# Gated linear attention and an MLP on one core: inputs turned by VectorE, four array tiles for the states, the MLP by 256 tokens and in quarter blocks at the start

## The chip, the cores and the metric

The kernel runs on one core of a Trainium2 chip. Its engines are TensorE (PE, matrix products), VectorE (DVE), ScalarE (ACT), GpSimd (POOL) and SyncE (SP), which here only issues DMAs. The metric is the device time of one execution in microseconds, as the median of several runs.

## The reference

The inputs are q, k, v and f_logit, each of 4 batches, 8 heads, 768 tokens and 48 values a head, and the MLP's weights w_in (384 x 2048) and w_out (2048 x 384), in 64-bit floats. The attention keeps a state per head, and the MLP takes the eight heads' outputs of a token side by side as its 384 inputs:

```
f = 1.0 / (1.0 + np.exp(-f_logit))
state = np.zeros((B, H, D, D), dtype=np.float32)
for t in range(S):
    state = f[:, :, t, :, None] * state + np.einsum('bhd,bhe->bhde', k[:, :, t], v[:, :, t])
    y[:, :, t] = np.einsum('bhd,bhde->bhe', q[:, :, t], state)
...
h = x @ w_in
g = h * (1.0 / (1.0 + np.exp(-1.702 * h)))
return (g @ w_out).astype(np.float32)
```

## The kernel before

**Units.** The 3072 tokens are cut into twelve units of 256 tokens, three to a batch. For each unit `attention` (L177) makes a list of parts, each a piece of the program with a kind, T or W. The MLP works on two units at a time (TM = 512 tokens, L399).

**Parts of a unit.** Six T parts turn f, q and k (`turn`, L187): `load_raw` (L143) brings them with tokens on partitions, in runs of 48 floats padded to 64. TensorE transposes 128x128 blocks with an identity (L195), four to a part, and ScalarE brings the result from PSUM, with a sigmoid for f (L201) and as a copy for q and k (L203), so that channels lie on partitions: two heads on 128 partitions, four such pairs side by side, 1024 columns in all. GpSimd multiplies f over pairs, fours and so on up to 64 tokens (L210). VectorE makes q times f (L214). Then come a first and a second W part and four W parts by `level` (L310). Each makes scores on TensorE (`score`, L220, matmul at L224); VectorE scales q and k up one level (`promote`, L251, at L260) and masks the scores while it takes them from PSUM (`evacuate`, L239, at L244); ScalarE copies keys (L264); TensorE adds the products with v (`add`, L269, at L273) into the PSUM tile py. Two T parts turn k back (`turn_k`, L324). A W part makes the sums of k and v for four chunks of 64 tokens (L347), and VectorE forms the states from them (L360 to L365). The last W part adds the states' share to py (L378): head h of a pair reads partitions of h and writes columns of h, so it is on two tiles of the array, while scores and adds use all four. ScalarE copies py to yT (L384), and ten DMAs put yT into xT (L390) with the MLP's inputs in their order on partitions.

**v.** `load_v` (L152) copies v to a buffer in DRAM with all heads of a token side by side, and then loads it seven times in the orders that the levels need (vl), and once in plain order (vn). There is one vl.

**MLP.** `mlp_h` (L401): for each of 16 blocks of 128 hidden values three matmuls (L412), a sigmoid on ScalarE (L418) and a product on VectorE (L419) into g. `mlp_o` (L422): for each 128 tokens sixteen matmuls (L429), a copy by ScalarE (L435) and a DMA out (L437). The hidden tiles, ph and po, share three PSUM banks.

**Weights.** They come as 64-bit floats in 24 pieces of w_in (256 columns) and 16 of w_out (384 columns). `load_weights` (L111) issues the DMA, of which three pieces can be in flight, and turns the bits into 32-bit floats with one ScalarE instruction (L130) and six on VectorE (L131 to L137).

**Order.** TensorE's instructions run in the order in which the program writes them (L81). The order on the other engines and on SP is made at compile time by a planner, which issues what is ready by its own costs, first the one that the program writes first. `merge` (L441) writes TensorE's order: after each part it takes a share of the fill, a list of MLP matmuls or of weight pieces. Units 0 and 1 take weight pieces as fill (L506, L508). The second half of unit 1 and unit 2 have the h matmuls of the first 512 tokens, in two halves of 256 (L509 to L514). From unit 3 on each unit takes one unit's worth of MLP, which lies a LAG behind (L515 to L520).

Of the kernel before, what the change touches and what calls it, by code (L numbers as in the profile page):

```python
# [24 lines left out]
def kernel(  # L25
# [44 lines left out]
    FG = 4  # L70
    NA = NP * U
# [16 lines left out]
    at = [wp.tile([P, 64], I32, tag="bits", name=f"at{j}", bufs=3) for j in range(2)]  # L88
# [8 lines left out]
    raw = const.tile([P, 3, NG, H, HS], F32, name="raw")  # L97
    for j in range(3):
        nc.vector.memset(raw[:, j, :, :, D:], 0.0)
# [3 lines left out]
    v_toks = [tc.dram_tile([U, DM], F32, name=f"v_tok{j}") for j in range(2)]  # L103

    WI, WO = 256, 384
    pieces_in = [(w_in[:, c, f:f + WI], moe_w_in[c * P:(c + 1) * P, f:f + WI])
                 for f in range(0, DFF, WI) for c in range(NK)]
    pieces_out = [(w_out[:, c, e:e + WO], moe_w_out[c * P:(c + 1) * P, e:e + WO])
                  for c in range(NFF) for e in range(0, DM, WO)]

    def load_weights(n, dst, src):  # L111

        w = dst.shape[1]
        if moe_w_in.dtype == F32:
            nc.sync.dma_start(out=dst, in_=src)
            return
        bits = wp.tile([P, w, 2], I32, tag="bits", name=f"bits_{n}", bufs=3)
        nc.sync.dma_start(out=bits.rearrange("p c two -> p (c two)"), in_=src.bitcast(I32))
# [24 lines left out]
    def load_raw(n):  # L143
        b, s0 = n // NU, n % NU * U
        for j, src in enumerate((f_logit, q, k)):
            for g in range(NG):
                nc.sync.dma_start(
                    out=raw[:, j, g, :, :D],
                    in_=src[b, :, s0 + g * G:s0 + (g + 1) * G, :].rearrange("h p d -> p h d"),
                )  # L150

    def load_v(n):  # L152
# [9 lines left out]
        for u, (m, half) in enumerate(V_HALF):  # L162
            nc.sync.dma_start(
                out=vl[:, u], in_=v_tok.rearrange("(n two m) e -> two n m e", two=2, m=m)[half]
            )
# [11 lines left out]
    def attention(n, loaded, xT, x0):  # L177
# [7 lines left out]


        def turn(j, a0):  # L187
            if not t:
                t["F"] = att.tile([P, NA], F32, tag="F", name=f"F_{n}")
                t["X"] = att.tile([P, 3, NA], F32, tag="X", name=f"X_{n}")  # L190
                t["tot"] = att.tile([P, NA], F32, tag="tot", name=f"tot_{n}")
            pt = ps.tile([P, 2, NG, P], F32, tag="tr", name=f"t{'fqk'[j]}_{n}_{a0}")
            for a in range(2):
                for g in range(NG):
                    nc.tensor.transpose(  # L195
                        pt[:, a, g, :], raw[:, j, g, 2 * (a0 + a):2 * (a0 + a + 1), :].rearrange("p h d -> p (h d)"), ident
                    )
            cols = slice(a0 * U, (a0 + 2) * U)
            src = pt.rearrange("p a g t -> p (a g t)")
            if j == 0:  # L200
                nc.scalar.activation(t["F"][:, cols], src, AF.Sigmoid)  # L201
            else:
                nc.scalar.copy(t["X"][:, 2 * (j - 1), cols], src)  # L203
            if j == 0 and a0:
                t["tms"], off = [t["F"]], 0
                for m in LEV:
                    nb = NA // (2 * m)
                    t2 = t["tms"][-1].rearrange("p (n two) -> p n two", two=2)
                    tn = t["tot"][:, off:off + nb]
                    nc.gpsimd.tensor_tensor(tn, t2[:, :, 0], t2[:, :, 1], ALU.mult)  # L210
                    t["tms"].append(tn)
                    off += nb
            if j == 1:
                nc.vector.tensor_tensor(t["X"][:, 1, cols], t["X"][:, 0, cols], t["F"][:, cols], ALU.mult)  # L214

        for j in range(3):
            for a0 in (0, 2):
                part("T")(lambda j=j, a0=a0: turn(j, a0))

# [9 lines left out]
        def tokens(j, m, half):  # L229
            return lambda h, x: t["X"][rows(h), j, x:x + G].rearrange("p (n two m) -> p n two m", two=2, m=m)[:, :, half, :]  # L230

        def keys(l):
            return lambda h, x: t["Kc"][rows(h), x // 2:x // 2 + 64]

# [16 lines left out]
        def promote(l):  # L251
# [5 lines left out]
            X = t["X"]  # L257
# [11 lines left out]
        def add(u, A, dst, start=False):  # L269

            for a in range(NP):
                for h, g in TILES:
                    nc.tensor.matmul(  # L273
                        dst(h, g, a), lhsT=t["vl"][g * 64:(g + 1) * 64, u, (2 * a + h) * D:(2 * a + h + 1) * D],
                        rhs=A(h, g, a), start=(start and a == 0), stop=False, skip_group_check=True,
                    )

        def half(m, hf):
            return lambda h, g, a: t["py"][rows(h), g, a, :].rearrange("p (n two m) -> p n two m", two=2, m=m)[:, :, hf, :]
# [5 lines left out]
        def _():  # L285
            t["vl"], t["vn"] = loaded()
            sc = scores()
            score(
                sc.rearrange("p h (a t) -> p h a t", a=NP), lambda h, x: t["X"][rows(h), 2, x:x + G:2],
                lambda h, x: view(t["X"], x, [[NA + 1, 2], [2, 64]])[rows(h)],  # L290
# [5 lines left out]
        def _():  # L296
            sc = scores()
            s4 = sc.rearrange("p h (s a t) -> p s h a t", s=2, a=NP)
            score(s4[:, 0], lambda h, x: t["X"][rows(h), 2, x + 1:x + G:2], lambda h, x: t["X"][rows(h), 0, x + 1:x + G:2])
# [5 lines left out]
                lambda h, g, a: t["py"][rows(h), g, a, :], start=True,  # L305
# [18 lines left out]
        def turn_k(a0):  # L324
            if a0 == 0:
                t["kn"] = att.tile([P, NP, NG, P], F32, tag="kn", name=f"kn_{n}")
            pt = ps.tile([P, 2, NG, P], F32, tag="tr", name=f"tkn_{n}_{a0}")
            for a in range(2):
                for g in range(NG):
                    x = (a0 + a) * U + g * G  # L330
                    nc.tensor.transpose(pt[:, a, g, :], t["X"][:, 2, x:x + G], ident)  # L331
# [37 lines left out]
        def _():  # L369
# [4 lines left out]
            for c in [1, 2, 3, 0][:NC - first]:  # L374
                for a in range(NP):
                    for h in range(2):
                        x = a * U + c * C
                        nc.tensor.matmul(  # L378
                            py[rows(h), c // 2, a, c % 2 * C:(c % 2 + 1) * C], lhsT=t["before"][c][rows(h), a],
                            rhs=t["X"][rows(h), 1, x:x + C], start=False, stop=True, skip_group_check=True,  # L380
                        )
            yT = att.tile([P, NP, NG, G], F32, tag="yT", name=f"yT_{n}", bufs=2)
            for h in range(2):
                nc.scalar.copy(yT[rows(h)].rearrange("p a g t -> p g a t"), py[rows(h)])  # L384
                for a in range(NP):
                    f0, f1 = (2 * a + h) * D, (2 * a + h + 1) * D
                    while f0 < f1:
                        end = min(f1, (f0 // P + 1) * P)
                        r0 = h * HS + f0 - (2 * a + h) * D
                        nc.sync.dma_start(  # L390
                            out=xT[f0 % P:f0 % P + end - f0, f0 // P, x0:x0 + U],
                            in_=yT[r0:r0 + end - f0, a].rearrange("p g t -> p (g t)"),
                        )
# [156 lines left out]
```

## Time and profile before

| | us |
|---|---|
| median of 3 runs | 797.74 |
| lowest, highest | 796.32, 798.1 |
| the profiled execution | 798.2 |
| its span, first to last instruction | 796.3 |
| TensorE busy | 722.1 |
| VectorE busy | 339.0 |
| ScalarE busy | 204.4 |
| GpSimd busy | 39.5 |

The profile is of one execution. Times within it are counted from the span's start. A line such as L429 is a line of the kernel; an arrow shows which tile an instruction writes and reads; a number after x is how many there are. Each fp32 matmul of the program shows as two instructions. Ends of matmuls are modelled, so their pace is read from the start of one to the start of the next.

### The profile page before, as it was taken

How to read it: one execution, taken by the hardware profiler on the slowest of the kernel's cores; microseconds unless marked ns; L12 is line 12 of the kernel's file. 1: busy time of each engine (PE TensorE's matmuls, PEld its weight loads, DVE VectorE, ACT ScalarE, POOL GpSimd, SP SyncE). 2: the span in 40 equal slices, each digit the busy share in tenths (PEclk: the TensorE clock that was granted, in tenths of full speed). 3: DMA queues.
4: the chain of work that ended last, by engine and by line, in shares of the span. 5: the costliest groups of instructions: out<-in, count | busy, mean ns of one | idle time of the engine just before them, and what ended most of it. 6: DMA issues, size and time to landing. Idle time of an engine off the chain costs nothing.

```text
span 796.3 us, 19489 instructions
## 1 busy us (share of the span) xinstructions
PE 722.1 (91%) x8672; PEld 447.8 (56%) x8672; DVE 339.0 (43%) x635; ACT 204.4 (26%) x357; POOL 39.5 (5%) x80
## 2 busy tenths in 40 slices
PE   3525498699999999999999999999999999999998
PEld 2423386486666555666555665555665556654454
DVE  4695898763524435313445233444134353102200
ACT  2223233323231242131242121331222331112100
POOL 2001000101010010010010010010010000000000
PEclk9997589899999999999999999999999999999999
DMA  9945836604564162271270370360350300100000
GB/s 188 200 119 161 192 98 190 139 2 121 82 150 61 46 129 28 72 130 31 70 120 3 99 122 12 92 100 2 116 84 12 110 2 12 31 21 0 0 21 20
DMA packets 130595, 63.39 MB, mean 80 GB/s; under 512 B 103888, under 2 KB 125392, under 8 KB 130512
## 3 DMA queue, kind: packets, MB, share of 16 engines
q1 hardware_dynamic: 130512, 62.15, 35.4%
q8 instruction: 68, 1.11, 0.6%
q14 instruction: 15, 0.12, 0.1%
HBM read 52.69 MB, written 9.44 MB: 78 GB/s over the span
## 4 chain that ended last, share of the span: by engine, by line
PE 82%; DVE 9%; DMA 4%; ACT 1%; issue 1%; SPq 1%; POOL 0%; DVEq 0%; ACTq 0%; POOLq 0%
PE o L429 32%; PE h L412 29%; PE sc L224 7%; PE y L273 5%; DMA bits<-in_moe_w_in_dram 3%; PE y L378 2%; DVE X L260 2%; PE tk L195 2%; PE tkn L331 1%; PE sc L347 1%; PE tq L195 1%; DVE s L133 1%; DVE a L136 1%; PE tf L195 1%; DVE A L244 1%
## 5 line engine op out<-in xcount | busy, mean ns | idle before, releaser
L412 PE MATMUL h<-xT,w_in 128*128 128x512 f32 (+1 forms) x672 | 273.1, 548 | 6.6 <-DMA xT<-yT 6.4
L429 PE MATMUL o<-w_out,g 128*128 128x384 f32 x768 | 265.8, 492 | 0.0
L429 PEld LDWEIGHTS o<-w_out,g 128*128 128x128 f32 x768 | 139.5, 190 | 86.0 <-issue 4.5
L412 PEld LDWEIGHTS h<-xT,w_in 128*128 128x128 f32 x672 | 124.0, 195 | 100.4 <-issue 82.6
L419 DVE TENSOR_TENSOR g<-h,sg 128x512 f32<-128x512 f32 (+1 forms) x112 | 68.6, 614 | 182.1 <-ACT sg L418 182.1
L260 DVE TENSOR_TENSOR X<-X,tot 128x1024 f32<-128x1024 f32 x60 | 73.3, 1222 | 86.3 <-PE sc L224 86.3
L418 ACT ACTIVATE sg<-h 128x512 f32<-128x512 f32 (+1 forms) x112 | 59.8, 535 | 115.3 <-PE h L412 115.2
L264 ACT COPY Kc<-X 128x512 f32<-128x512 f32 x60 | 37.6, 627 | 177.8 <-DVE X L260 177.8
L224 PE MATMUL sc<-X,Kc 48*64 48x64 f32 x1920 | 44.8, 235 | 22.3 <-DVE A L244 17.5
L273 PE MATMUL y<-A,vl 64*48 64x64 f32 (+1 forms) x2688 | 64.7, 241 | 0.0
L224 PEld LDWEIGHTS sc<-X,Kc 48*64 48x64 f32 x1920 | 37.1, 145 | 49.0 <-issue 28.8
L244 DVE TENSOR_TENSOR A<-sc,masks 128x512 f32<-128x512 f32 (+1 forms) x84 | 62.8, 759 | 0.0
L273 PEld LDWEIGHTS y<-A,vl 64*48 64x48 f32 x2688 | 55.0, 130 | 6.8 <-issue 6.4
L210 POOL TENSOR_TENSOR tot<-F 128x512 f32<-128x512 f32 x12 | 12.6, 1048 | 593.9 <-ACT F L201 593.9
L384 ACT COPY yT<-y 48x1024 f32<-48x1024 f32 x24 | 24.1, 1006 | 59.4 <-PE y L378 50.9
L435 ACT COPY osb<-o 128x384 f32<-128x384 f32 x24 | 11.5, 478 | 101.0 <-PE o L429 100.1
L224 PE MATMUL sc<-X 48*64 48x128 f32 (+1 forms) x768 | 24.9, 272 | 12.0 <-DVE A L244 12.0
L224 PEld LDWEIGHTS sc<-X 48*64 48x64 f32 x768 | 19.9, 148 | 25.7 <-issue 24.7
L362 DVE TENSOR_TENSOR st<-st,tot 128x192 f32<-128x192 f32 x44 | 15.7, 357 | 41.4 <-POOL tot L210 40.1
L130 ACT ACTIVATE a<-bits 128x256 f32<-128x256 f32 (+1 forms) x40 | 19.2, 486 | 51.3 <-DMA bits<-in_moe_w_in_dram 24.3
L195 PE MATMUL tq<-ident,raw 128*128 128x128 f32 x96 | 17.3, 310 | 12.2 <-ACT F L201 10.7
L365 DVE TENSOR_TENSOR st<-st,sc 128x192 f32<-128x192 f32 x44 | 15.5, 353 | 25.2 <-PE sc L347 24.1
(39 smaller groups left out, 387.8 us busy)
## 6 DMA issues: line engine op xcount, KB each, us to landing
vl<-v_tok SPq DMA_DIRECT2D x84, 192.0 KB
bits<-in_moe_w_in_dram SPq DMA_DIRECT2D x24, 256.0 KB
bits<-in_moe_w_out_dram SPq DMA_DIRECT2D x16, 384.0 KB
raw<-in_f_logit_dram SPq DMA_DIRECT2D x24, 192.0 KB
raw<-in_q_dram SPq DMA_DIRECT2D x24, 192.0 KB
raw<-in_k_dram SPq DMA_DIRECT2D x24, 192.0 KB
v_tok<-in_v_dram SPq DMA_DIRECT2D x12, 384.0 KB
vn<-v_tok SPq DMA_DIRECT2D x12, 384.0 KB
```

Source lines behind the costliest of these rows:

```text
L130: nc.scalar.activation(a, hi.bitcast(F32), AF.Abs, scale=2.0 ** 112)
L195: nc.tensor.transpose(pt[:, a, g, :], raw[:, j, g, 2 * (a0 + a):2 * (a0 + a + 1), :].rearrange("p h d -> p (h d)"), ident)
L224: nc.tensor.matmul(out[g * HS:(g + 1) * HS, h, a, :], lhsT=lhs(h, a * U + g * G), rhs=rhs(h, a * U + g * G), start=True, stop=True,)
L244: nc.vector.tensor_tensor(A[:, :, c:c + w].rearrange("p h (x t) -> p h x t", t=64), t["sc"][:, :, c:c + w].rearrange("p h (x t) -> p h x t ...
L260: nc.vector.tensor_tensor(qk, qk, by, ALU.mult)
L264: nc.scalar.copy(Kc.rearrange("p (n m) -> p n m", m=m), X[:, 2].rearrange("p (n two m) -> p n two m", two=2, m=m)[:, :, 0, :],)
L273: nc.tensor.matmul(dst(h, g, a), lhsT=t["vl"][g * 64:(g + 1) * 64, u, (2 * a + h) * D:(2 * a + h + 1) * D], rhs=A(h, g, a), start=(start a ...
L384: nc.scalar.copy(yT[rows(h)].rearrange("p a g t -> p g a t"), py[rows(h)])
L412: nc.tensor.matmul(ph[:, :T], lhsT=w_in[:, n, ff * P:(ff + 1) * P], rhs=xTs[s][:, n, t0:t1], start=(n == 0), stop=(n == NK - 1),)
L418: nc.scalar.activation(sg[:, :T], ph[:, :T], AF.Sigmoid, scale=1.702)
L419: nc.vector.tensor_tensor(g[ff // FG][:, ff % FG, t0:t1], ph[:, :T], sg[:, :T], ALU.mult)
L429: nc.tensor.matmul(po, lhsT=g[ff // FG][:, ff % FG, tt * P:(tt + 1) * P], rhs=w_out[:, ff, :], start=(ff == 0), stop=(ff == NFF - 1),)
```

## The change

- **Turning.** `load_raw` now loads f, q and k so that partition i of a group of 32 holds eight tokens in a row of one head, 1.5 KB at a time, in four DMAs for each of the three. Groups 0 and 2 hold the rows from their start, groups 1 and 3 from the 32nd value on, so each row is read twice. `turn` is one VectorE instruction on 128x1024 that transposes 32x32 blocks and writes the columns in order of tokens (a step of eight words). F and X are now single tiles for the whole kernel. `begin` turns f and q, takes the sigmoid, has GpSimd make the products and issues the next loads; `begin_k` makes q times f as one instruction and turns k. Both for the next unit are written around the last part of the present one.
- **States.** In py the two heads of a pair change places for the second 128 tokens (`columns`), and the last part takes the chunks in pairs (1, 2), (3, 0), so that the states' matmuls visit four array tiles.
- **xT.** There is one xT for each unit. Its order of inputs on partitions is other (96 of three pairs of heads, and the fourth pair split in three), w_in's rows are loaded to match, and twelve DMAs of 128 columns replace ten of 256. `load` of the next v is written behind them.
- **MLP.** It goes by units of 256 tokens. ph, po and the tile of `turn_k` share four PSUM banks.
- **Weights.** They come in four rounds of three pieces of w_in (512 columns) and four of w_out (384). The DMA is issued four pieces ahead of the conversion.
- **Start.** Unit 0 has round 0's conversions and no fill, unit 1 has round 1's and the first quarter block of unit 0's MLP, unit 2 rounds 2 and 3 and the other seven quarter blocks of units 0 and 1 but for a LAG. A quarter block (`mlp_block`) is four blocks of h and their share of o, which ScalarE copies to a sum (first round) or VectorE adds to it.

```diff
+    raw = const.tile([P, 3, NP, R * D], F32, name="raw")
...
+    for r in range(NGR):
+        for c in range(NK):
+            f = slice(r * WG, (r + 1) * WG)
+            pieces.append((w_in[:, c, f], [(slice(0, D2), moe_w_in[c * D2:(c + 1) * D2, f]),
+                                           (slice(D2, P), moe_w_in[NK * D2 + c * DR:NK * D2 + (c + 1) * DR, f])]))
+        for c in range(r * FG, (r + 1) * FG):
+            pieces.append((w_out[:, c, :], [(slice(0, P), moe_w_out[c * P:(c + 1) * P, :])]))
...
+        src = (f_logit, q, k)[j]
+        for r in range(4):
+            lo = 32 * (r % 2)
+            nc.sync.dma_start(
+                out=raw[32 * r:32 * (r + 1), j, :, :R * D - lo],
+                in_=src[b, r // 2::2, s0:s0 + U, :].rearrange("a (i j) d -> i a (j d)", j=R)[:, :, lo:],
+            )
...
-        for j in range(3):
-            for a0 in (0, 2):
-                part("T")(lambda j=j, a0=a0: turn(j, a0))
+        def turn(j, out):
+            nc.vector.transpose(
+                out.rearrange("p (a i j) -> p a j i", a=NP, j=R),
+                raw[:, j].rearrange("p a (j d) -> p (a j) d", j=R)[:, :, :32],
+            )
+
+        def begin():
+            turn(0, F)
+            nc.scalar.activation(F, F, AF.Sigmoid)
+            turn(1, X[:, 0])
+            t["tot"] = att.tile([P, NA], F32, tag="tot", name=f"tot_{n}")
...
+            if n + 1 < NALL:
+                load_raw(n + 1, 0)
+                load_raw(n + 1, 1)
+
+        def begin_k():
+            nc.vector.tensor_tensor(X[:, 1], X[:, 0], F, ALU.mult)
+            turn(2, X[:, 2])
+            if n + 1 < NALL:
+                load_raw(n + 1, 2)
...
+        def columns(h, g):
+            return rows(h ^ g)
...
+            pt = ps.tile([P, 2, NG, P], F32, tag="mm", name=f"tkn_{n}_{a0}", bufs=4)
...
-            for c in [1, 2, 3, 0][:NC - first]:
+            for cs in ((1, 2), (3, 0)):
                 for a in range(NP):
-                    for h in range(2):
+                    for c in cs:
+                        if t["before"][c] is None:
+                            continue
+                        for h in range(2):
+                            x = a * U + c * C
+                            nc.tensor.matmul(
+                                py[columns(h, c // 2), c // 2, a, c % 2 * C:(c % 2 + 1) * C],
+                                lhsT=t["before"][c][rows(h), a], rhs=X[rows(h), 1, x:x + C],
+                                start=False, stop=True, skip_group_check=True,
+                            )
...
+    def parts_of(n, pieces=(), by=1.0):
+        parts = list(units[n][2])
         if n + 1 < NALL:
+            parts.insert(-1, ("-", units[n + 1][0]))
+            parts.append(("-", units[n + 1][1]))
+        todo, out, at = list(pieces), [], 0
+        total = sum(kind == "W" for kind, _ in parts)
+        for kind, fn in parts:
+            out.append((kind, fn))
+            at += kind == "W"
+            while todo and len(pieces) - len(todo) < len(pieces) * at / (by * total):
+                i = todo.pop(0)
+                out.append(("-", lambda i=i: (convert_weights(i), fetch_weights(i + PIECES_AHEAD))))
...
+    UNIT = NFF * NK * U + U // P * NFF * DM
+    LAG = 18 * DM
...
+    merge(parts_of(0, block(0)), [], 0, steady)
+    fill = mlp_block(0, 0)
+    merge(parts_of(1, block(1)), fill, UNIT // NGR, steady)
+    for u, r in ((0, 1), (1, 0), (1, 1), (0, 2), (1, 2), (0, 3), (1, 3)):
+        fill += mlp_block(u, r)
+    merge(parts_of(2, block(2, 2), by=0.75), fill, 2 * UNIT - UNIT // NGR - LAG, steady)
+    for n in range(2, NALL):
+        fill += mlp_unit(n)
     for n in range(3, NALL):
+        merge(parts_of(n), fill, UNIT, steady)
```

282 lines of the change are left out of this document (127 added, 155 removed).

## The prediction

> **What bounds the kernel now.** I read the page first (span, slices), then busy time by stage, then TensorE's instructions in order of time, the chain, and the groups of instructions. From the page:
>
> ```profile
> span 796.3 us, 19489 instructions
> ...
> PE   3525498699999999999999999999999999999998
> ...
> DVE  4695898763524435313445233444134353102200
> ```
>
> A slice is 20 us. From the tenth slice on, TensorE is full and VectorE a third to a half used; in the first nine it is the other way round. So there are two stages. I cut the span where unit 0's scores begin, where its states' part ends, where unit 1's ends, where unit 2's ends and unit 3 begins, and where the last unit ends:
>
> ```profile
> 0.00:19.91 19.91, 6.86 (x24) 4.27 (x25) 8.98 (x29) 5.70 (x10) 4.50 (x14) 1.00 0.97 187
> 19.91:67.95 48.04, 21.38 (x570) 18.56 (x570) 40.87 (x119) 11.24 (x23) 0.00 (x0) 1.00 0.68 156
> 67.95:134.40 66.45, 45.15 (x693) 36.21 (x694) 55.34 (x136) 23.03 (x47) 3.48 (x6) 0.71 0.63 160
> 134.40:188.45 54.05, 45.30 (x716) 36.60 (x716) 33.24 (x68) 18.14 (x37) 3.24 (x6) 0.89 0.40 95
> 188.45:685.58 497.13, 496.17 (x6374) 295.33 (x6372) 189.47 (x270) 131.35 (x217) 28.33 (x54) 1.00 0.33 70
> 685.58:796.30 110.72, 107.19 (x301) 56.85 (x300) 11.07 (x16) 14.91 (x25) 0.00 (x0) 0.99 0.05 16
> ```
>
> (Columns: stage, length, busy PE, PEld, DVE, ACT, POOL, clock, DMA share, GB/s.) DVE is busy 40.87 of 48.04 us in unit 0 and 55.34 of 66.45 in unit 1; from 188.45 on TensorE never rests. Gains must come from TensorE's own work after 188.45, or from an earlier start before it. What a piece of that work costs is read where TensorE is full, from start to start, since the printed ends are modelled:
>
> ```profile
> 452.62 1.99 PE L378 MATMUL y<-X,st 48*48 48x64 f32 x64
> 454.55 4.14 PE L429 MATMUL o<-w_out,g 128*128 128x384 f32 x12
> 458.52 0.60 PE L195 MATMUL tf<-ident,raw 128*128 128x128 f32 x4
> 458.96 1.46 PE L429 MATMUL o<-w_out,g 128*128 128x384 f32 x4
> 460.25 0.60 PE L195 MATMUL tf<-ident,raw 128*128 128x128 f32 x4
> ...
> 480.96 1.08 PE L273 MATMUL y<-A,vl 64*48 64x64 f32 x64
> 481.96 4.14 PE L429 MATMUL o<-w_out,g 128*128 128x384 f32 x12
> ```
>
> and from pieces of the chain:
>
> ```profile
> 57.94 1.14 DVE X L260
> ...
> 710.29 41.20 PE h L412 x96
> 751.49 41.30 PE o L429 x128
> ...
> 792.85 0.48 ACT osb L435
> ```
>
> One h of 512 columns takes 41.20/96 = 0.429 us, one o 41.30/128 = 0.323. MLP of 512 tokens is 82.5 us, of a unit (256) 41.25, of all twelve 495. Two units in the full stage:
>
> ```profile
> 337.44:452.69 115.25, 115.25 (x1426) 68.09 (x1428) 43.01 (x61) 30.54 (x50) 6.86 (x12) 1.00 0.35 72
> ```
>
> So attention costs TensorE (115.25 - 82.5)/2 = 16.4 us a unit.
>
> **The change, part by part: the full stage.** *Turning.* Four transposes occupy 458.52 to 458.96, 0.44 us (the four o behind them take 1.29, which is 4 x 0.323, so nothing else is hidden there). Six such groups of a unit go: 2.64, with a change of tile 2.7 us. The ScalarE copies of q and k go too; ScalarE is used 30.54 of 115.25 us, so that buys nothing.
>
> *States.* 64 matmuls on two array tiles take 454.55 - 452.62 = 1.93 us; 64 of the same length that rotate over four tiles (L273) take 481.96 - 480.96 = 1.00. Gain 0.93 us. Bounds: nothing, to 0.93. I take 0.93, as the order a, c, h visits four tiles in turn like L273's.
>
> [...]
>
> *MLP by 256.* The same columns in twice the instructions. The first block already runs at 256 columns:
>
> ```profile
> 170.27 1.99 PE L412 MATMUL h<-xT,w_in 128*128 128x256 f32 x8
> 172.20 0.69 PE L224 MATMUL sc<-X,Kc 48*64 48x64 f32 x32
> ...
> 173.27 2.42 PE L412 MATMUL h<-xT,w_in 128*128 128x256 f32 x10
> 175.62 0.69 PE L224 MATMUL sc<-X,Kc 48*64 48x64 f32 x32
> ```
>
> Eight take 1.93 us, ten 2.35: 0.21 each, half of 0.429. So no loss on TensorE. On DVE:
>
> ```profile
> L419 DVE TENSOR_TENSOR g<-h,sg 128x512 f32<-128x512 f32 x80 | 55.3, 691 | 167.6 <-ACT sg L418 167.6
> L419 DVE TENSOR_TENSOR g<-h,sg 128x256 f32<-128x256 f32 x32 | 13.3, 420 | 14.5 <-ACT sg L418 14.5
> L260 DVE TENSOR_TENSOR X<-X,tot 128x1024 f32<-128x1024 f32 x60 | 73.3, 1222 | 86.3 <-PE sc L224 86.3
> L210 POOL TENSOR_TENSOR tot<-F 128x512 f32<-128x512 f32 x12 | 12.6, 1048 | 593.9 <-ACT F L201 593.9
> L135 DVE TENSOR_SCALAR a<-s 128x384 int32<-128x384 int32 x16 | 5.6, 352 | 0.1
> L137 DVE TENSOR_TENSOR w_out<-a,s 128x384 f32<-128x384 f32 x16 | 8.8, 550 | 0.1
> ```
>
> A unit has 16 x 420 = 6.7 us of g instead of 8 x 691 = 5.5. Three turns on DVE are new, each 128x1024 f32. No such row exists. Below: a one-source operation on SBUF does 384 in 352 ns (L135), so 0.9 us for 1024. Above: the slowest elementwise rate is POOL's, 1048 ns for 512, so 2.1 us. I take L260's 1.22 (same shape, same engine, one element at a time), 1.14 where DVE is full: the chain shows L260 at 1.14 beside its mean of 1.222, so neighbours overlap by 0.08. The two X products become one of L260's size. DVE in the full stage: 43.0/2 + 3 x 1.22 + 1.2 = 26 us of some 54, hidden beside TensorE. It also falls well: begin and begin_k land in the o part of the fill, where no g waits behind them. If turn k is late, the next unit's first score is late; the cover is the 3/26 of the fill behind the states' part, 4.8 us, against one product and one turn, 2.4.
>
> [...]
>
> So a unit costs 41.25 + 16.4 - 2.7 - 0.93 = 54.0 us where it was 57.6.
>
> *xT.* Twelve DMAs of 512 B rows replace ten of 1 KB:
>
> ```profile
> 138.53 7.16 SPq L390 DMA_DIRECT2D xT<-yT x10
> ...
> 144.77 2.20 PE L412 MATMUL h<-xT,w_in 128*128 128x256 f32 x4 [6.37 <-DMA xT<-yT]
> ```
>
> Issue goes from 7.2 to 8.6 us, and xT is there 144.77 - 134.40 = 10.4 us after the states' part, now about 12. The fill behind that point is 4.8 + LAG's 18 calls (11.6 us) plus two score parts: some 20 us, and 16.4 behind the last unit. Hidden. The 32 loads and moves that SP now issues a unit, at 0.4 to 0.7 us, make 17 of 54 us.
>
> *v's loads* are now written behind the twelve xT DMAs, not ahead of the states' part. Issued there, v_tok would land 14 us after the states' part and vl 3 later, where the second score part's products want vl after 4.8 + 1.3 + 4.8 + 1 = 12: a wait of 5 us a unit. But SP's order is the planner's:
>
> ```profile
> 181.56 4.67 SPq L163 DMA_DIRECT2D vl<-v_tok  x7
> ...
> 193.25 0.61 SPq L156 DMA_DIRECT2D v_tok<-in_v_dram  x1
> 193.91 7.42 SPq L390 DMA_DIRECT2D xT<-yT  x10
> ```
>
> The v_tok at 193.25 is unit 4's, written in unit 3, and stands ahead of unit 2's xT: loads go out when their tile is free. vl is freed by the last products, a part ahead of the states'. Cost nothing, at worst 5 us.
>
> **The front.** The clock column reads 1.00 in the first 68 us, yet 32 scores there take twice what they take later, so I use the early spacings for units 0 and 1:
>
> ```profile
> 19.91 1.99 PE L224 MATMUL sc<-X 48*64 48x128 f32 x32
> ...
> 468.99 1.14 PE L224 MATMUL sc<-X 48*64 48x128 f32 x32
> ```
>
> *Start.* raw moves twice the bytes (each row is read at two offsets, 2.3 MB a unit) in packets of 1.4 to 1.5 KB for 192 B:
>
> ```profile
> 6.00:9.00 3.00, 1.33 (x5) 0.72 (x4) 0.00 (x0) 0.60 (x1) 0.00 (x0) 1.00 1.52 164
> 10.60:12.60 2.00, 0.00 (x0) 0.00 (x0) 0.09 (x1) 0.09 (x1) 0.00 (x0) 1.00 1.07 318
> ```
>
> 164 GB/s with 192 B, 318 when 2 KB weight rows move: 7.1 us either way. f is first in the queue and one weight piece stands before q, not three and v. f lands near 5.5, k near 11.5; a turn behind it gives unit 0's first score at 13, not 19.91.
>
> *Unit 0.* By the rows a level is a score (0.9), L260 (1.14) and an evacuation half L260's size (0.6) with their waits, about 3 us; two first parts at 4.5, four levels at 3 and 8 for tkn, sums and states come to 29 us, and it took 48 with 17 pieces converted between: 1.1 us a piece. With seven to nine: 37 us, ends at 50, not 67.95.
>
> *Unit 1.* xT(0) is there at 62, and the first h stands right behind the first score: a wait of 7 us that was not there. Then seven parts, each DVE's 1.7 plus 2.2 us of conversion and an h: 4.8 us; with tkn and states it ends at 97, against 134.40.
>
> *Unit 2.* TensorE has 1.75 x 41.25 - 11.6 = 60.6 us of MLP and 12.7 of attention. DVE has 14 pieces (each three like L135 and three like L137, less 0.08 each: 384 columns 2.2 us, 512 by columns 2.8; 35 in all), 18 of attention with turns, 28 g at 0.34, 5 of sums: 68. Two engines both nearly full: I add 7 to TensorE's 73 and 3 for X and k, so unit 3 begins at 97 + 3 + 73 + 7 = 180. Bounds: 158 (TensorE full from the first h at 62: 70.9 of MLP, two attentions of 12.7) and 200 (unit 0 as long as before, 11 more; unit 2 at 1.2 times its busier engine, as the stage from 67.95 was: 88).
>
> **Sum.** Of before: 188.45, MLP left 495 - 41.2 = 453.8, nine attentions at 16.4 = 147.4, the end behind the last o 796.3 - 792.8 = 3.5: 793.2, 3.1 short of the span. After: 180; MLP done by then 41.25 x 2 - 11.6 = 70.9, left 424.1; nine at 12.75 = 114.7; 3.5; 3.1: 725. The profiled execution took 798.2 for its span of 796.3, and the median is 797.74, so 1.4 is added: **727**. Of the 71 us, 33 are TensorE's own work, 38 the front (8 earlier with 30 more of MLP done).
>
> **Rivals.** *Turns at 2.1 us* (DVE bounds the front): eleven of them before unit 3, 0.96 more each: 738. For: DVE is full there. Against: behind 188.45 it has room. [...]
>
> *A wait in the full stage.* An h now lasts 1.29 us and its bank is freed through ACT and DVE; four banks are shared with tkn. Where DVE is busy with a product and an evacuation (1.8), the cover is 3.9. If it fails, two h a unit, 2.5 us, nine times: 749; with v's loads behind xT, 5 us: 772. Against: DVE is half idle, and the planner put loads early.
>
> *States still at 1.93:* the four-tile part does not do what it says; 11 x 0.93: 737.
>
> *Slower:* a turn that takes several passes. Each turn stands on DVE ahead of the next unit's scores. The front pays 11 (T - 1.14), and beyond 3.6 us (the 4.8 of cover less a product) every unit waits, 9 (T - 3.6). That reaches 71 us at T = 5.8 us; at 6 it gives 802. Against: five times L260, where POOL's slow rate is under twice.
>
> **Chances.** Forecast 0.62 (its own range 705 to 747, from the front's 158 to 200), slow turns 0.18, wait 0.10, states 0.04, slower 0.06. The range is 704 to 760: the front's low bound, and above it slow turns with the front's high bound (758) and the wait of 2.5. A measurement here tells 0.2%, 1.6 us, from no change: faster 0.93, same 0.01, slower 0.06.
>
> **What would show it.** Units 54 us apart; 64 L378-type matmuls in 1.0 us; a turn's row near 1.22 us; first scores near 13 us; unit 0's end near 50, the first h at 62 behind a DMA; unit 3's start near 180; TensorE full from there. A turn over 2.1, idle TensorE after 180 or units over 56 us apart would make it wrong.

## The result and the profile after

The kernel after takes **761.5 us** (median of 4 runs, 760.7 to 763.1) where the kernel before took 797.6 in the same comparison. The ratio is 0.955, with a 95% interval of 0.953 to 0.957. It is faster, as forecast, but by half: the forecast was 727 us with a range of 704 to 760. One run of the first experiment below, at 795.1 us, fell into a slower state of the chip and is left out; every other time is of the fast state.

The page of the kernel after has the span and TensorE's busy share in 40 slices of 19 us:

```profile
span 761.1 us, 20034 instructions
...
PE   0551577879999999999999999999999999999998
```

The full stage now begins at 214.40 us, 26 us later than the 188.45 of before, and the fourth slice of TensorE has a hole (a 1) that no slice of before had. Below, the span is cut into stages: to unit 0's first score, to the end of unit 0's states, to the first h, to the end of unit 1's states, to unit 3's first score, and on into the last unit. The columns are stage, length, busy PE, PEld, DVE, ACT, POOL, clock, DMA share and GB/s.

```profile
0.00:19.87 19.87, 0.00 (x1) 0.00 (x1) 12.82 (x22) 3.56 (x4) 4.99 (x14) 1.00 0.94 208
19.87:54.20 34.33, 19.80 (x568) 17.25 (x568) 24.32 (x39) 6.59 (x10) 0.11 (x1) 0.75 0.80 183
54.20:82.77 28.57, 2.02 (x35) 1.65 (x33) 27.04 (x50) 7.37 (x11) 3.57 (x6) 0.52 0.48 117
82.77:122.50 39.73, 28.44 (x590) 20.66 (x590) 25.33 (x47) 8.70 (x17) 0.04 (x1) 0.80 0.75 173
122.50:214.40 91.90, 82.85 (x827) 58.98 (x823) 69.96 (x139) 26.01 (x51) 7.25 (x12) 0.90 0.64 148
214.40:662.00 447.60, 447.38 (x6066) 330.94 (x6066) 232.92 (x338) 116.50 (x229) 22.56 (x48) 1.00 0.36 91
```

From 214.40 on TensorE is full, at the full clock, and that stage is the one that was forecast. All but 1.3 us of the miss lies before it, and most of it in 54.20:82.77, where TensorE works 2.02 of 28.57 us. TensorE's instructions in order of time show what it waits for (start, busy time, what, and in brackets the idle time ahead of it with its releaser):

```profile
19.87 1.98 PE L251 MATMUL sc<-X 48*64 48x128 f32 x32 [19.87 <-DVE X L219]
...
60.63 1.99 PE L251 MATMUL sc<-X 48*64 48x128 f32 x32 [6.39 <-DVE X L219]
82.77 2.90 PE L452 MATMUL h<-xT,w_in 128*128 128x256 f32 x6 [20.16 <-DMA xT<-yT]
89.59 1.96 PE L304 MATMUL y<-A,vl 64*48 64x128 f32 x32 [2.70 <-DMA vl<-v_tok]
101.87 0.87 PE L304 MATMUL y<-A,vl 64*48 64x64 f32 x18 [4.39 <-issue]
...
124.92 1.98 PE L251 MATMUL sc<-X 48*64 48x128 f32 x32 [0.78 <-DVE X L242]
...
214.40 1.15 PE L251 MATMUL sc<-X 48*64 48x128 f32 x32
...
432.62 1.15 PE L251 MATMUL sc<-X 48*64 48x128 f32 x32
...
481.30 1.11 PE L412 MATMUL y<-X,st 48*48 48x64 f32 x64
482.35 4.78 PE L468 MATMUL o<-w_out,g 128*128 128x384 f32 x14
487.06 1.15 PE L251 MATMUL sc<-X 48*64 48x128 f32 x32
```

The first h waits 20 us for unit 0's xT. What holds xT up? The copy that it is made from is done early; then come SP's instructions of the same profile:

```profile
54.28 2.02 ACT L420 COPY yT<-y 48x1024 f32<-48x1024 f32 x2 [4.91 <-PE y L412]
```

```profile
41.49 24.10 SPq L139 DMA_DIRECT2D bits<-in_moe_w_in_dram  x6
69.02 0.35 SPq L139 DMA_DIRECT2D bits<-in_moe_w_out_dram  x1
69.41 1.86 SPq L177 DMA_DIRECT2D raw<-in_f_logit_dram  x4
...
73.21 0.72 SPq L423 DMA_DIRECT2D xT<-yT  x1
...
82.02 0.59 SPq L186 DMA_DIRECT2D v_tok<-in_v_dram  x1
```

yT is ready at 56.3, but the first xT DMA is issued at 73.2. Ahead of it on SP stand weight loads of the second round, which take from 41.5 to 65.6 to issue (nothing at all goes out from 42.3 to 62.9) and then one more at 69.0: they wait for a free `bits` tile, of which there are four. Behind these, and still ahead of xT, are eight DMAs for unit 2's f and q (3.8 us). Behind xT, in turn, stands v. The wait's releaser, in the waits of SP from 0 to 220 us, is the last use of those tiles (total, how often, longest):

```profile
SPq L139 <- DVE a L165: 57.3, 13, 20.5
```

And the last use is late because of the order on the engines that convert. These are two of VectorE's instructions, one behind the other:

```profile
58.47 2.01 DVE L219 STREAM_TRANSPOSE X<-raw 128x1024 f32<-128x1024 f32 x1
60.33 0.34 DVE L160 TENSOR_SCALAR s<-bits 128x384 int32<-128x384 int32 x1
```

The last conversions of the first round (L160 on) stand behind unit 1's turns and start only at 60.3; ScalarE's part of them (L159) stands behind its copy to yT and starts at 56.3. SP's next load goes out at 62.88, as the first of them has read its tile (62.80). So a chain of places in order runs from VectorE's turns through a conversion, a `bits` tile and SP's queue to xT, a chain that the prediction's sum didn't have.

Against the forecast's own marks, all in us:

| stage | forecast | after | difference |
|---|---|---|---|
| to unit 0's first score | 13 | 19.9 | +6.9 |
| unit 0, to the end of its states | 37 | 34.3 | -2.7 |
| then to unit 2's first score | 50 | 70.7 | +20.7 |
| unit 2 | 80 | 89.5 | +9.5 |
| from unit 3's first score to the end | 545.4 | 546.7 | +1.3 |
| span | 725.4 | 761.1 | +35.7 |

(The forecast's 50 is unit 1 to 97 and its 3 us for X and k.)

### The profile page after: what moved, and what is told of

Same layout as the page of the kernel before. It is cut to its first block, busy times and chain, and to the rows that moved or that the text cites. A ratio compares the mean times of both kernels' runs of the same rounds, so it can differ in the third digit from the quotient of the medians.

```text
span 761.1 us, 20034 instructions
## 1 busy us (share of the span) xinstructions
PE 676.3 (89%) x8864; PEld 499.3 (66%) x8864; DVE 415.4 (55%) x679; ACT 188.2 (25%) x365; POOL 38.5 (5%) x80
## 4 chain that ended last, share of the span: by engine, by line
PE 79%; DVE 9%; DMA 6%; SPq 2%; issue 2%; POOL 0%; ACT 0%; DVEq 0%; POOLq 0%; ACTq 0%
PE h L452 32%; PE o L468 31%; PE sc L251 6%; PE y L304 5%; DMA raw<-in_q_dram 2%; DMA bits<-in_moe_w_out_dram 2%; PE sc L378 1%; PE tkn L362 1%; DVE X L290 1%; DMA bits<-in_moe_w_in_dram 1%; PE y L412 1%; DVE a L165 1%; DVE s L162 1%; DMA v_tok<-in_v_dram 1%; DVE A L275 1%
## 5 line engine op out<-in xcount | busy, mean ns | idle before, releaser
L452 PE MATMUL h<-xT,w_in 128*128 128x256 f32 x1152 | 271.8, 388 | 20.2 <-DMA xT<-yT 20.2
L452 PEld LDWEIGHTS h<-xT,w_in 128*128 128x128 f32 x1152 | 216.7, 193 | 55.4 <-issue 21.5
L468 PEld LDWEIGHTS o<-w_out,g 128*128 128x128 f32 x768 | 144.3, 193 | 101.6 <-DVE g L458 7.7
L458 DVE TENSOR_TENSOR g<-h,sg 128x256 f32<-128x256 f32 x192 | 81.0, 423 | 167.8 <-ACT sg L457 167.8
L457 ACT ACTIVATE sg<-h 128x256 f32<-128x256 f32 x192 | 73.6, 384 | 176.8 <-PE h L452 176.7
L304 PEld LDWEIGHTS y<-A,vl 64*48 64x48 f32 x2688 | 52.9, 126 | 18.9 <-issue 12.6
L219 DVE STREAM_TRANSPOSE X<-raw 128x1024 f32<-128x1024 f32 x24 | 49.2, 2051 | 16.0 <-PE sc L251 11.9
L290 DVE TENSOR_TENSOR X<-X,F 128x1024 f32<-128x1024 f32 x12 | 14.7, 1226 | 38.7 <-PE sc L251 38.7
L159 ACT ACTIVATE a<-bits 128x384 f32<-128x384 f32 (+1 forms) x28 | 16.8, 609 | 48.5 <-DVE w_out L166 22.2
L219 DVE STREAM_TRANSPOSE F<-raw 128x1024 f32<-128x1024 f32 x12 | 24.3, 2025 | 4.6 <-DMA raw<-in_f_logit_dram 4.6
L242 DVE TENSOR_TENSOR X<-X,F 128x1024 f32<-128x1024 f32 x12 | 15.4, 1286 | 17.6 <-PE y L412 17.6
```

The source lines that it names most:

```text
L159: nc.scalar.activation(a, hi.bitcast(F32), AF.Abs, scale=2.0 ** 112)
L219: nc.vector.transpose(out.rearrange("p (a i j) -> p a j i", a=NP, j=R), raw[:, j].rearrange("p a (j d) -> p (a j) d", j=R)[:, :, :32],)
L290: nc.vector.tensor_tensor(qk, qk, by, ALU.mult)
L304: nc.tensor.matmul(dst(h, g, a), lhsT=t["vl"][g * 64:(g + 1) * 64, u, (2 * a + h) * D:(2 * a + h + 1) * D], rhs=A(h, g, a), start=(start a ...
L452: nc.tensor.matmul(ph, lhsT=w_in[:, c, ff * P:(ff + 1) * P], rhs=xTs[n][:, c, :], start=(c == 0), stop=(c == NK - 1))
L457: nc.scalar.activation(sg, ph, AF.Sigmoid, scale=1.702)
```

## The experiments

The theory after the result: xT is late because of what stands ahead of it on SP. The rivals: VectorE is simply too full in the front (conversions, or turns of 2.05 us), or the array tiles or the turning bring less than they seem to.

### xT issued by ScalarE

```diff
-                    nc.sync.dma_start(out=xT[h * D:(h + 1) * D, :, cols], in_=yT[rows(o), :NK, g])
+                    nc.scalar.dma_start(out=xT[h * D:(h + 1) * D, :, cols], in_=yT[rows(o), :NK, g])
...
-                        nc.sync.dma_start(
+                        nc.scalar.dma_start(
```

> The twelve xT DMAs of a unit are issued by ScalarE right behind its copy to yT, not by SP. Theory (SP's queue): the first h waits 20.2 us because xT(0), whose yT is ready at 56.3, stands on SP behind weight loads that wait for a free bits tile; without them xT lands near 66 to 70 and the kernel takes 745 to 752 us. Rival (VectorE): in that wait VectorE is busy 27.0 of 28.6 us with conversions that are needed anyway, so an earlier h only moves the wait: 757 to 762 us.

781.8 us (778.7 to 788.9), a ratio of 0.982 (0.976 to 0.989): above both expectations, and some 20 us slower than the kernel after. TensorE in order of time:

```profile
65.73 2.90 PE L452 MATMUL h<-xT,w_in 128*128 128x256 f32 x6 [2.76 <-DMA xT<-yT]
...
88.66 1.96 PE L304 MATMUL y<-A,vl 64*48 64x128 f32 x32 [13.93 <-DMA vl<-v_tok]
```

xT is there 17 us sooner, which confirms that its place on SP, and not yT or the transfer, made it late. But v stays behind the weights on SP, and the wait comes back as 13.9 us for vl. Unit 3 begins at 223.30, later than the 214.40 of the kernel after. In the full stage, where the kernel after doesn't wait, TensorE now waits for keys, because ScalarE, which copies them, has twelve DMAs a unit to issue. Waits of TensorE from 300 to 600 us:

```profile
PE sc L251 <- ACT Kc L294: 7.9, 5, 2.7
```

From unit 3's first score to the end it loses 17 us (563.7 for 546.7), and 11.2 of them are this wait. So the expected gain was more than taken by new waits. The queue that a DMA leaves and the one that it enters both count.

### Turns that write side by side

```diff
-                out.rearrange("p (a i j) -> p a j i", a=NP, j=R),
+                out.rearrange("p (a j i) -> p a j i", a=NP, j=R),
```

The tokens of a unit then stand in another order; the work is the same.

> The turn writes its 32-word rows side by side and not eight words apart, so tokens come out in another order within a unit (the computation is then of permuted tokens). Theory (the write's step costs): a turn falls from 2.05 to about 1.2 us; eleven turns stand before unit 3, so the kernel takes 752 to 757 us. Rival (the transposition itself costs): a turn stays at 2.0 us and the time within 760 to 763.

758.5 us (755.6 to 759.5), a ratio of 0.952 (0.949 to 0.954): 3 us less, between the two expectations. The groups of VectorE's instructions, first of the kernel after and then of this one (count, busy time, mean ns, idle time ahead):

```profile
L219 DVE STREAM_TRANSPOSE X<-raw 128x1024 f32<-128x1024 f32 x24 | 49.2, 2051 | 16.0 <-PE sc L251 11.9 <-PE tkn L362 4.1
```

```profile
L219 DVE STREAM_TRANSPOSE X<-raw 128x1024 f32<-128x1024 f32 x24 | 29.9, 1244 | 21.8 <-PE sc L251 17.4 <-PE tkn L362 4.1 <-DMA raw<-in_k_dram 0.3
```

A turn costs 1.24 us when it writes runs of 32 words and 2.05 when it writes single words eight apart. The step is the whole of the difference to the 1.22 that the prediction took. Yet the first h still waits 20.5 us for xT, as without the edit. The price of the turn was wrong, but it isn't what most of the time was lost to.

### States on two array tiles

```diff
-            return rows(h ^ g)
+            return rows(h)
...
-                    h, cols = o ^ g, slice(g * G, (g + 1) * G)
+                    h, cols = o, slice(g * G, (g + 1) * G)
```

> The two heads keep their columns, so the states' 64 matmuls visit two array tiles as in the kernel before; all else is as in the changed kernel. Theory: they take 1.93 us and not 1.04, nine times in the full stage and twice before it: 769 to 772 us. Rival (hidden): 760 to 763.

769.0 us (766.2 to 772.7), a ratio of 0.965 (0.961 to 0.969). Two first scores, one unit apart:

```profile
433.56 1.14 PE L251 MATMUL sc<-X 48*64 48x128 f32 x32
...
488.86 1.14 PE L251 MATMUL sc<-X 48*64 48x128 f32 x32
```

The spacing is 55.30 us, where the kernel after has 487.06 - 432.62 = 54.44. The four tiles are worth 0.86 us in a unit, close to the 0.93 forecast.

### Weights copied, not converted

```diff
-        nc.scalar.activation(a, hi.bitcast(F32), AF.Abs, scale=2.0 ** 112)
-        ve.tensor_scalar(si, hi, -(1 << 31), -(1 << 31), op0=ALU.bitwise_and, op1=ALU.bitwise_xor)
...
-        ve.tensor_tensor(dst, a, s, ALU.add)
+        nc.vector.tensor_copy(dst, hi.bitcast(F32))
```

Each weight piece is one copy of the high words instead of seven instructions; the conversion is left out.

> Each weight piece is copied by one VectorE instruction (its high words) in place of one ScalarE and six VectorE instructions, so the weights' values are not the right ones. Theory (SP's queue): tiles for weight loads come free sooner, the wait of 20 us for xT(0) goes and little else: 737 to 745 us. Rival (VectorE bounds the whole front): all of some 57 us of VectorE's work that is left out shows there: 705 to 725 us.

749.3 us (747.5 to 752.4), a ratio of 0.940 (0.937 to 0.943): above both expectations. With nearly all of VectorE's conversion work gone, the first h still comes late (the lines of this kernel stand 16 higher). SP's row, then TensorE's:

```profile
41.32 21.08 SPq L139 DMA_DIRECT2D bits<-in_moe_w_in_dram  x6
```

```profile
79.62 2.90 PE L436 MATMUL h<-xT,w_in 128*128 128x256 f32 x6 [17.02 <-DMA xT<-yT]
```

The weight loads block SP for 21 us instead of 24, since the copies stand on VectorE where the conversions stood, behind unit 1's turns. From the end of unit 0's states (51.80) to this h VectorE is busy 12.14 of 27.82 us. So it isn't the amount of VectorE's work that makes xT late but its order. That rules out the rival of a VectorE that is simply full for this wait. The 12 us that were gained come in the main from elsewhere in the front: in the profiled executions the first h is 3.1 us earlier, unit 2's first score 9.0 and unit 3's 14.1.

### The second round's weight loads behind the first xT

Pieces 7 to 10 are issued on SP behind unit 0's last xT.

```diff
-                    nc.sync.dma_start(out=xT[h * D:(h + 1) * D, :, cols], in_=yT[rows(o), :NK, g])
+                    last["xT"] = nc.sync.dma_start(out=xT[h * D:(h + 1) * D, :, cols], in_=yT[rows(o), :NK, g])
...
-                out.append(("-", lambda i=i: (convert_weights(i), fetch_weights(i + PIECES_AHEAD))))
+                out.append(("-", lambda i=i: (convert_weights(i), i + PIECES_AHEAD in late or fetch_weights(i + PIECES_AHEAD))))
...
+        def rest():
+            with tc.issue_after(last["xT"].ins):
+                for i in late:
+                    fetch_weights(i)
...
-    merge(parts_of(0, block(0)), [], 0, steady)
+    merge(parts_of(0, block(0), late=range(7, 11)), [], 0, steady)
```

> Round 1's first four weight pieces (7 to 10) are issued on SP behind unit 0's xT and v(1), not ahead of them; nothing else moves. Theory (SP's queue): xT(0) goes out at about 57 instead of 73, the first h starts near 69 instead of 82.8, v(1) follows (second add near 78 instead of 89.6), and unit 1 is some 10 us shorter: 748 to 755 us. Rival (the weights are what is late): round 1's pieces land later by as much as xT lands sooner, and unit 2 gives it back: 758 to 764.

757.9 us (755.0 to 760.6), a ratio of 0.949 (0.946 to 0.953), between the two expectations and next to the rival's. The first h comes at 66.4 instead of 82.8, but only 3.6 us of those 16 reach the end. In order of time:

```profile
66.42 2.90 PE L452 MATMUL h<-xT,w_in 128*128 128x256 f32 x6 [3.90 <-DMA xT<-yT]
73.49 1.96 PE L304 MATMUL y<-A,vl 64*48 64x128 f32 x32 [3.00 <-DMA vl<-v_tok]
...
110.91 0.46 PE L412 MATMUL y<-X,st 48*48 48x64 f32 x4 [7.58 <-DVE st L396]
...
119.04 1.98 PE L251 MATMUL sc<-X 48*64 48x128 f32 x32 [2.91 <-DVE X L242]
...
137.88 1.96 PE L304 MATMUL y<-A,vl 64*48 64x128 f32 x32 [6.92 <-DMA vl<-v_tok]
...
211.27 1.15 PE L251 MATMUL sc<-X 48*64 48x128 f32 x32
```

Most of it is given back in unit 1 already, whose end comes only 5.9 us earlier: TensorE waits 7.58 us for states that stand on VectorE behind conversions of the second round, which now begin at 94.2 instead of 68.9, much as the rival had it. In unit 2 the wait for vl is 6.92 us where it was 2.62, and the unit lasts 211.27 - 119.04 = 92.2 us. v's loads are still written behind xT.

### The same, with v's loads ahead of the states' part

```diff
             last["st"] = st
+            if n + 1 < NALL:
+                load(n + 1)
...
-            if n + 1 < NALL:
-                load(n + 1)
```

This edit comes on top of the one above.

> As e2_hold, and the loads of the next v are written ahead of the states' part, as in the kernel before, so that they stand ahead of xT on SP in every unit. Theory: the waits of the second score part's adds for vl (2.7 us in unit 1, 2.6 in unit 2, and more in unit 1 of e2_hold) go too: 743 to 750 us. Rival (xT is now late by v's seven issues, 4 to 5 us): no better than e2_hold.

**743.6 us** (742.6 to 746.1), a ratio of 0.932 (0.929 to 0.934), 18 us below the kernel after. In order of time:

```profile
71.90 2.90 PE L451 MATMUL h<-xT,w_in 128*128 128x256 f32 x6 [9.77 <-DMA xT<-yT]
...
114.35 1.99 PE L251 MATMUL sc<-X 48*64 48x128 f32 x32 [0.50 <-DVE X L242]
...
194.17 1.15 PE L251 MATMUL sc<-X 48*64 48x128 f32 x32
```

No wait for vl is left, and unit 2 lasts 194.17 - 114.35 = 79.8 us, the prediction's 80, where it was 89.5. The first h is 5.5 us later than without this edit: xT leaves SP at 62.75, behind v's loads and those of unit 2's f and q, where it left at 57.63. The span is 740.8.

### v's loads alone

Only the second of the two edits; the weight loads stay ahead of xT.

> Only the place of the next unit's loads is changed: written before the states' part, as in the kernel before; the weight pieces of the second round stay ahead of the first xT. If the place of v's loads costs something by itself, the waits for vl in units 1 and 2 go (2.7 and 2.6 us at their starts, more inside) and the time is 752 to 758 us. If the first xT alone sets the front, v's place is worth nothing while xT waits to 82.8 us, and the time is 759 to 764 us; the 18 us of the run with both edits then need both.

763.0 us (760.7 to 765.9), a ratio of 0.958 (0.954 to 0.961): no gain, as the second theory had it. In order of time:

```profile
95.79 2.90 PE L451 MATMUL h<-xT,w_in 128*128 128x256 f32 x6 [33.40 <-DMA xT<-yT]
...
132.14 1.99 PE L251 MATMUL sc<-X 48*64 48x128 f32 x32 [1.26 <-DVE X L242]
...
212.06 1.15 PE L251 MATMUL sc<-X 48*64 48x128 f32 x32
```

v now goes first, and xT, which is behind the weights, behind v and behind unit 2's f and q, comes 13 us later still. But unit 2 is 212.06 - 132.14 = 79.9 us. The four kernels together:

| | weights ahead of the first xT | weights behind it |
|---|---|---|
| v behind xT | 761.5 us; first h 82.8; unit 2 89.5 | 757.9 us; first h 66.4; unit 2 92.2 |
| v ahead of the states' part | 763.0 us; first h 95.8; unit 2 79.9 | 743.6 us; first h 71.9; unit 2 79.8 |

Alone the edits bring 3.6 and -1.5 us (the second is within the spread of the runs), together 17.9. Each one by itself leaves xT or v late; unit 2's length goes by v's place.

### A later fill

On top of the 743.6 us kernel, unit 1's MLP fill begins only at its fourth part, so that the scores don't stand behind the first h on TensorE.

```diff
-    def merge(parts, fill, columns, share):
+    def merge(parts, fill, columns, share, skip=0):
+        parts = [(kind if i >= skip else '-', fn) for i, (kind, fn) in enumerate(parts)]
...
-    merge(parts_of(1, block(1)), fill, UNIT // NGR, steady)
+    merge(parts_of(1, block(1)), fill, UNIT // NGR, steady, skip=3)
```

> As e7_hold_v, and unit 1 takes its share of MLP only from its fourth part on, so that its first three score parts do not stand behind an h that waits for xT(0). Theory (TensorE's written order costs what is left of the wait, 7 us by the prediction): 737 to 745 us. Rival (VectorE sets unit 1's pace): no change against e7_hold_v.

744.0 us (742.1 to 747.9), no change. TensorE's wait of 9.8 us for xT is gone, and it waits for VectorE instead:

```profile
68.93 1.13 PE L251 MATMUL sc<-X 48*64 48x64 f32 x32 [6.01 <-DVE A L275]
...
107.72 0.45 PE L414 MATMUL y<-X,st 48*48 48x64 f32 x4 [10.32 <-DVE st L396]
```

VectorE is busy 47.77 of the 54.35 us from unit 1's first score to unit 2's, and from 97.3 to 107.3 it does nothing but conversions, ahead of the states that TensorE waits for. With the queue in order, VectorE sets unit 1's pace.

### The first weight piece behind f, q and k

```diff
-    fetch_weights(0)
     load_raw(0, 1)
     load_raw(0, 2)
     load(0)
-    for i in range(1, PIECES_AHEAD):
+    for i in range(PIECES_AHEAD):
```

> Only the first weight piece's load is moved, behind the loads of q, k and v of unit 0. Theory (start): q and k land some 2 us sooner and the conversion of 5 us no longer stands between the turns of f and q on VectorE, so the first score starts near 15.5 instead of 19.9, and the kernel gains as much: 756 to 759 us. Rival (the first piece's conversion is only moved into unit 0's chain): 760 to 763.

758.2 us (756.6 to 759.1), a ratio of 0.949 (0.947 to 0.951). The first score comes at 14.70 instead of 19.87; 3.3 of these 5.2 us reach the end. In the kernel after, VectorE takes the first piece's conversion between f's turn and q's:

```profile
7.17 2.02 DVE L219 STREAM_TRANSPOSE F<-raw 128x1024 f32<-128x1024 f32 x1 [4.64 <-DMA raw<-in_f_logit_dram]
9.62 0.43 DVE L160 TENSOR_SCALAR s<-bits 128x512 int32<-128x512 int32 x1 [0.43 <-DMA bits<-in_moe_w_in_dram]
...
14.61 2.00 DVE L219 STREAM_TRANSPOSE X<-raw 128x1024 f32<-128x1024 f32 x1
```

### All three edits of order, without and with side by side writes

Two kernels: the 743.6 us kernel with the edit above, and the same with the turn's edit (the output's tokens then stand in another order).

> Three edits of order together: the second round's weight loads behind the first xT, v's loads ahead of the states' part, and the first weight piece's load behind the first unit's q, k and v. If the gains add (18 us for the first two, 3 us for the third), the time is 738 to 743 us, with unit 3's first score at 189 to 192 us. If the weights, which now start 5 us later, become the next wait for the MLP of unit 0, the third gain is lost and the time is 743 to 747 us.

744.0 us (741.2 to 745.1): the gain at the start is lost. The time is the one that the second theory gave, but the wait is another: not the MLP of unit 0 waits for the weights, but its attention. The first score is at 14.80, but unit 1's first score at 59.34 instead of 60.15. The longest new wait stands in unit 0 (4.63 us, where the 743.6 us kernel has 0.83):

```profile
33.95 1.13 PE L251 MATMUL sc<-X,Kc 48*64 48x64 f32 x32 [4.63 <-ACT a L159]
```

L159 is ScalarE's part of a conversion, whose weight piece now comes later; ScalarE holds it ahead of a copy of keys.

> The same three edits, with the turn's words written side by side (the tokens of a unit then stand in another order, so that the output is a permuted one); a turn is 1.24 us instead of 2.05. If the turn's price shows once the order of loads no longer does, the three turns in a row ahead of a unit's scores are shorter in the first three units: 3 x 0.8 us in each, some 5 to 8 us below the run without it, 731 to 737 us. If VectorE's time is still covered, it is 0 to 3 us, as it was with the loads in the changed kernel's order.

**740.1 us** (740.0 to 741.5), a ratio of 0.928 (0.927 to 0.930): 3.9 us less, between the two expectations. The profiled executions differ by 1.2 us of span only (739.4 and 738.2), so how much of the 3.9 is the turn isn't settled. It is no more than some 4 us. It leaves the tokens in another order; of the kernels that keep the reference's order, the one at 743.6 us and the two at 744.0 can't be told apart.

## Why the prediction was right or wrong

**Right: the stage where TensorE is full.** The forecast was 54.0 us a unit; it is 54.44. The states' matmuls take 482.35 - 481.30 = 1.05 us (1.00 forecast), and the experiment with two tiles costs 0.86 us a unit. The 256-column h cost nothing, the turning of 2.7 us is gone, and from unit 3's first score on the forecast was 545.4 us against 546.7. That VectorE and the xT transfers are hidden there is right too: between 214.40 and 662.00 TensorE is busy 447.38 of 447.60 us.

**Wrong: the xT of unit 0, "there at 62", and "a wait of 7 us".** This was the largest failure, with what hangs on it: 20.7 us between unit 0's end and unit 2's start. The first h comes 28.6 us after the states' part (54.20 to 82.77), where about 12 were forecast. The transfer was judged rightly: issued by ScalarE, xT is there at 65.73, some 11 us after that run's states' part. The step that failed is the one on SP's order: "loads go out when their tile is free", taken from a row of the full stage where v's load stood ahead of xT, so that both xT's wait for its turn on SP and v's place were costed at nothing. In the front the planner puts weight loads ahead of xT whose tile is not yet free, and a waiting DMA holds up all behind it on SP (the 24.10 us of the row at 41.49). I had counted what SP issues in a unit (17 of 54 us), not what waits in its queue. The four kernels in the table show it, and that both loads had to be moved: with both in place unit 2 is 79.8 us and the front is 14 us over the forecast instead of 34.

**Wrong: unit 2 at 80.** "Cost nothing, at worst 5 us" for v's loads was worked out for the full stage; in unit 2 their place is worth 9.6 us, of which 2.62 is the wait for vl itself. The working was right with v in time (79.8 and 79.9). The kernel after against the 743.6 us kernel, over unit 2 from first score to first score:

```profile
124.92:214.40 89.48, 81.20 (x821) 58.48 (x821) 67.54 (x136) 23.78 (x49) 4.91 (x11) 0.91 0.63 145
```

```profile
114.35:194.17 79.82, 77.67 (x820) 56.40 (x820) 67.65 (x137) 23.70 (x50) 4.89 (x11) 0.96 0.63 150
```

VectorE does the same 67.6 us in both. TensorE idles 8.3 us in the one and 2.2 in the other, and the same instructions take 3.5 us longer at the lower clock (0.91 for 0.96).

**Wrong: the start at 13.** It came at 19.87. The step "7.1 us either way" with "one weight piece stands before q" counted that piece as a transfer and forgot its conversion, which VectorE puts between the turns. The experiment that moves the piece gains 5.2 us; 1.1 of it is f's turn, which starts at 6.07 for 7.17, which leaves some 4 for the conversion. The side by side write gives 14.80 - 14.05 = 0.75 more, so 1.05 us is left for the transfers. The rate was also too high: 318 GB/s was assumed, and the first 19.87 us of the kernel after move 208 at a share of 0.94.

**Wrong in size: the turn at 1.22 us.** It is 2.05, near the upper bound of 2.1 and within the range that was kept. The destination's step makes the difference: single words eight apart give 2051/1024 = 2.0 ns a value, adjacent words 1244/1024 = 1.2. The rival with a price of 2.1 us (738 us in all) took 0.96 us for each of eleven turns; the dense write, which takes 0.81 us off each, brought 3.0 and 3.9 us, not the 8.9 of eleven turns. The rival's mechanism, a front that VectorE alone bounds, is not what happened.

**The other rivals.** The wait in the full stage (749 or 772) and the states at 1.93 (737) did not occur. The slower case needed 5.8 us a turn. One reading of the profile's page was too simple, though nothing in the sum rests on it: not all of the first nine slices of before have VectorE as the busier engine, since the prediction's own table gives TensorE 45.30 and VectorE 33.24 of 54.05 us in the last stage of the front.

**What stays open.** With all in order the front is still 14 us over the forecast (unit 3 at 194.17, not 180): 7 at the start, 10 in unit 1, less 2.7 in unit 0. In unit 1 the first h comes at 71.9 rather than 62. Unit 0 ends 4.3 us later than forecast, and xT still stands on SP behind v and behind unit 2's f and q: yT is ready at 56.4 and xT's first DMA leaves at 62.75. Behind that h VectorE sets the pace. Kernels that put xT ahead of those loads too, or the states ahead of the second round's conversions, were not tried.

## What to carry to other kernels

When DMAs share one issuing queue, list for each what stands ahead of it and which of those wait for a buffer: a load issued ahead of need, whose buffer is not free, delays everything that stands behind it (here six weight loads took 24.10 us to issue, and xT's first DMA left 16.9 us after yT was ready), and moving one load may only change which one is late. Where an order is made by a planner, a row from the steady stage doesn't settle the order in the start, where other loads are in play. And where two loads hold each other up, an edit that moves one of them has to be measured together with its partner: here two edits brought 3.6 and -1.5 us alone and 17.9 together.

## What was not expected of the hardware

**A wait that cost more than its length.** In unit 2 of the kernel after a wait of 4.34 us on TensorE is followed by slow work. In order of time, and then, by windows, the clock in the stretch of these ten o and in the one after it:

```profile
159.09 6.08 PE L468 MATMUL o<-w_out,g 128*128 128x384 f32 x10 [4.34 <-DVE g L458]
```

```profile
159.09:165.15 6.06, 6.06 (x11) 3.37 (x12) 6.00 (x15) 1.73 (x3) 0.00 (x0) 0.57 0.75 193
165.15:175.00 9.85, 9.85 (x155) 7.53 (x157) 8.70 (x18) 4.04 (x9) 0.00 (x0) 1.00 0.40 113
```

From start to start these ten o take 5.92 us (the next row begins at 165.01) at a granted clock of 0.57, where fourteen take 4.71 at 1.00 (482.35 to 487.06 above), so 3.36 for ten. The wait took 4.3 us, and the ten o behind it some 2.6 more than at 1.00. The length of the wait alone doesn't settle it: over the other kernels, waits of 3.16 to 9.14 us ahead of ten such o are followed by 5.18 to 6.43 us for the ten, and waits of up to 1.82 by 3.49, but one wait of 3.32 us (in the kernel with v's loads alone) is followed by 3.49 as well. What set the clock was not tested. The forecast had no such term; behind this one wait it is 2.6 us.

**Waits that nothing in the profile explains.** In the front, TensorE stops for about 4 us in the middle of a group with "issue" as the only reason: the row at 101.87 above has 4.39, and its y products for "issue" sum to 8.4 us in the first 220 us. Their sum differs between the kernels (2.7 to 8.4 us), but one of them stands ahead of the same two products of unit 0 in all twelve kernels with the change (0.22 to 4.60 us); the kernel before has none of them. The one at 101.87 stands where the DMA share is 1.04 (from 98 to 103 us); their cause wasn't tested.
